# Two experts that begin with the first tokens, order edges on the transposes of experts' tokens, and the last two units tile by tile

## The chip, the cores and the metric

The kernel runs on one core of a Trainium2 chip. Its time is the device time of one execution in microseconds. A core has five engines, each with its own in-order queue of instructions: TensorE (PE, with its weight loads as PEld), VectorE (DVE), ScalarE (ACT), GpSimd (POOL) and SyncE (SP), which here only issues DMA transfers. GpSimd issues the indirect ones, gathers and scatters of rows. They wait for each other through semaphores.

## The reference, cut to what matters

Three layers follow each other on 2304 tokens of 512 features.

```python
# attention: 4 batches x 8 heads, 576 x 64; only the 32 largest scores of a row are kept
x = attention(q, k, v)                       # 2304 x 512
# dense layer
h = x @ w_in;  g = h * clip(h + 3, 0, 6) / 6
x = g @ w_out                                # 2304 x 2048 and back to 512
# mixture of 8 experts: each token goes to its two best by noisy logits
logits = x @ w_gate + log1p(exp(x @ w_noise)) * noise
top2, top2_w = two largest of each row, softmax over the two
for e in range(8):
    mask = tokens that chose e
    out[mask] += top2_w * (relu(x[mask] @ w1[e]) @ w2[e])    # 512 -> 1024 -> 512
```

## The kernel before, in words

The first part (`phase_a`) runs attention and the dense layer together, in steps written out by hand, for chunks of two token tiles of 128. A unit of the dense layer is one block of 128 of the 2048 inner features for one chunk: `mm1` (line 462, tile `h`, 12 matmuls), then a ReLU, a product and a split on ScalarE, VectorE and GpSimd, then `mm2` (line 502, tile `xa`, 6 matmuls). Weights of 11 of the 16 blocks are streamed again for every chunk (tag `ws`, 4 buffers, shared with the experts' raw weights `r`), five stay (tag `wr`, shared with the experts' converted weights). Every number is split into a rounded part and a remainder, so a product takes three matmuls. When a chunk is done, its tokens are routed (`make_route`): a small chain on GpSimd, VectorE and ScalarE ends in scatters of token numbers and gate weights into a table `idw` in memory (line 755), one region for each expert. The routing runs in groups of tiles; the last group is tiles 16 and 17.

The second part (`phase_b`) runs the experts. A job is one expert and a range of rows of its region: `jobs` holds (expert, first row, tiles). With EARLY = 1 there are nine: expert 0 with its first 384 rows (3 tiles), expert 0 with the next 256 (2 tiles), and experts 1 to 7 with 5 tiles each. A job below EARLY is *early*: it reads rows that the first 16 token tiles wrote and does not wait for the last two. A flag checks that every early expert has its 384 rows by then; otherwise a general path runs at the end.

A job has eight units, one for each block of 128 of the 1024 inner features. Unit `g` is made of: `wload` (two DMAs of 256 KB on SP, three units ahead), `wsplit` (a copy on ScalarE, line 859, and a subtraction, line 861, on VectorE for the first four jobs and on GpSimd for the others), `mm1` (line 875, tile `hb`, in one PSUM buffer of two banks, tag "s"), ReLU and low part into `hh` (lines 880 and 881), and `mm2` (line 895, tile `ac`, one accumulator bank for each token tile, three matmuls for each tile). A job's tokens come by `fetch`: a DMA reads `idw` (line 830), GpSimd gathers the rows (line 810) into one of two buffers `xg`, and `turn` (lines 841 to 845) transposes one tile: four transposes on TensorE, a copy on ScalarE, a subtraction on VectorE. `turn` of an early job uses the PSUM buffer "s", that of other jobs the bank "misc". In the program, `turn` of the next job's tile j stands in unit 3 + j of this one. `finish` scales the accumulators by the gate weight, adds what other jobs wrote (`old`, gathered from `out`), and scatters the rows to `out` (line 912); jobs below `fresh` need no `old`. From unit 20 on (`LOOK`) each unit also checks one or two pieces of `w_in` and `w_out` for very small values: a DMA of 256 KB and two VectorE instructions (lines 978 to 981), ordered behind that unit's low part.

The framework sets each engine's order: it simulates the program with a cost model, and gives a free engine the ready instruction that stands first in the program. `after(tc, o, before)` adds an edge for this order alone; on the chip nothing waits for it, but an engine's queue is in order.

Of the kernel before, what the change touches and what calls it, by code (L numbers as in the profile page):

```python
# [141 lines left out]
def phase_a(tc, pools, ident, q, k, v, w_in, w_out, X, thrs, wscr, stream, begin, on_chunk=None, slots=NSLOT, pace=None):  # L142
    nc = tc.nc
    wp, ap, mp, ps, dr = pools
# [295 lines left out]
    chunks = [list(range(t, min(t + 2, slots // 8))) for t in range(0, slots // 8, 2)]  # L440
    chunk_of = {t: (c, j) for c, ts in enumerate(chunks) for j, t in enumerate(ts)}
    W, HP, G, ACC = {}, {}, {}, {}

    def w_fetch(u):
        c, fb = u
# [7 lines left out]
    def mm1(u):  # L453
        c, fb = u
        n = 128 * len(chunks[c])
        w = W[u][:, :, 0:512].rearrange("p a (d f) -> p a d f", d=4)
        xt = XT[c]
        p = ps.tile([128, 512], F32, name=f"h{c}_{fb}", tag="h")
        m = 0
        for d in range(4):  # L460
            for a, b in ((0, 0), (0, 1), (1, 0)):
                nc.tensor.matmul(p[:, 0:n], w[:, a, d, :], xt[b][:, d, 0:n], start=(m == 0), stop=(m == 11))  # L462
                m += 1
        HP[u] = p

    R = {}

# [37 lines left out]
    XM, XW = {}, []  # L505
# [10 lines left out]
    fill = []  # L516
# [18 lines left out]
    for st in range(-6, end):  # L535
# [13 lines left out]
        s_, a, b, c, d, e, av_, x1, x2 = (st - x for x in (OS, OA, OB, OC, OD, OE, OV, OX, OY))  # L549
# [47 lines left out]
        while fill and room > 0:  # L597
            room -= fill[0][0]
            fill.pop(0)[1]()
    return fill, XW  # L600


NE, DF2 = 8, 1024
NF2 = DF2 // 128
# [2 lines left out]
CAP0 = 384  # L607
AHEAD = 3
LOOK = 20
EARLY = 1  # L610
DVE_JOBS = 4
NOID = 1 << 20
SCW = 2
# [6 lines left out]
def after(tc, o, before):  # L620
    tc.add_manual_dep(o.ins, before.ins.name, mybir.DependencyInfo(
        mybir.DependencyClass.NoSync, mybir.DependencyReason.SCHED_ONLY), reason="order")
# [159 lines left out]
    return on_chunk, scat, (nz, tok, logits, logits2, route)  # L782


def phase_b(tc, pools, ident, X, idw, w1, w2, out, early, late, looks):


    nc = tc.nc
    wp, bp, ps = pools
# [5 lines left out]
    XE, ID, ACC, WT, HH, RAW = {}, {}, {}, {}, {}, {}  # L795
    accs = ["pa", "av", "h", "xa0", "xa1"]
    xg = [bp.tile([128, NJ, DM], F32, name=f"xg{i}") for i in range(2)]
# [36 lines left out]
    def turn(job, j):  # L834
        xe = XE[job]
        if job < EARLY:
            pm = ps.tile([128, 2, 512], F32, name=f"et{job}_{j}", tag="s")[:, 0]
        else:
            pm = ps.tile([128, 512], F32, name=f"et{job}_{j}", tag="misc")
        for d in range(4):  # L840
            nc.tensor.transpose(pm[:, d * 128:(d + 1) * 128], xg[job % 2][:, j, d * 128:(d + 1) * 128], ident)  # L841
        pv = pm.rearrange("p (d n) -> p d n", d=4)
        sl = slice(j * 128, (j + 1) * 128)
        nc.scalar.copy(xe[:, 0, :, sl], pv)
        TT(xe[:, 1, :, sl], pv, xe.bitcast(F32)[:, 0, :, sl], op=ALU.subtract)  # L845
# [18 lines left out]
    def mm1(g):  # L864
        job, f = divmod(g, NF2)
        n = 128 * jobs[job][2]
        w = WT[g][:, :, 0:512].rearrange("p a (d f) -> p a d f", d=4)
        p = ps.tile([128, 2, 512], F32, name=f"hb{g}", tag="s")
        nh = 1 if n <= 512 else 2
        hn = n // nh  # L870
        for half in range(nh):
            m = 0
            for d in range(4):
                for a, b in ((0, 0), (0, 1), (1, 0)):
                    nc.tensor.matmul(p[:, half, 0:hn], w[:, a, d, :], XE[job][:, b, d, half * hn:(half + 1) * hn],  # L875
                                     start=(m == 0), stop=(m == 11))
                    m += 1
        h = bp.tile([128, 2, CAP], F32R, name=f"hh{g}", tag="hh", bufs=2)
        hv = h[:, :, 0:n].rearrange("p a (b n) -> p a b n", b=nh)
        nc.scalar.activation(hv[:, 0], p[:, 0:nh, 0:hn], AF.Relu)  # L880
        LOW[:] = [STT(hv[:, 1], p[:, 0:nh, 0:hn], 0.0,  # L881
                      h.bitcast(F32)[:, :, 0:n].rearrange("p a (b n) -> p a b n", b=nh)[:, 0],
                      op0=ALU.max, op1=ALU.subtract)]
        HH[g] = h

    def mm2(g):
        job, f = divmod(g, NF2)
        w = WT.pop(g)[:, :, 512:1024]
        h = HH.pop(g)
        prev = None  # L890
        for j in range(jobs[job][2]):
            if f == 0:
                ACC[job, j] = ps.tile([128, 512], F32, name=f"ac{job}_{j}", tag=accs[(j + 3 * (jobs[job][1] > 0)) % 5])
            for m, (a, b) in enumerate(((0, 0), (0, 1), (1, 0))):
                o = nc.tensor.matmul(ACC[job, j], h[:, a, j * 128:(j + 1) * 128], w[:, b, :],  # L895
                                     start=(f == 0 and m == 0), stop=(f == NF2 - 1 and m == 2))
                if g == N - 1:

                    if prev: after(tc, o, prev)
                    prev = o  # L900

    def finish(job):
        e, _, nj = jobs[job]
# [16 lines left out]
    N = len(jobs) * NF2  # L920
# [7 lines left out]
    for g in range(N):  # L928
        job, f = divmod(g, NF2)
# [247 lines left out]
def body(tc, q, k, v, w_in, w_out, w_gate, w_noise, noise, w1, w2, out, dbg=None):  # L1177
    nc = tc.nc
    with ExitStack() as ctx:
        cp = ctx.enter_context(tc.tile_pool(name="cp", bufs=1))  # L1180
        wp = ctx.enter_context(tc.tile_pool(name="wp", bufs=1))
        dr = ctx.enter_context(tc.tile_pool(name="dr", bufs=1, space=bass.MemoryType.DRAM))
        ps = ctx.enter_context(tc.tile_pool(name="ps", bufs=1, space=bass.MemoryType.PSUM))
        ident = cp.tile([128, 128], F32, name="ident")
        make_identity(nc, ident)
        thrs = cp.tile([128, NSLOT], F32, name="thrs")
        cnt = cp.tile([128, NE], F32, name="cnt")
        few = cp.tile([128, 1], F32, name="few")
        tiny = cp.tile([128, 64], F32, name="tiny") if w_in.dtype != F32 else None
        X = dr.tile([NTOK, DM], F32, name="X")  # L1190
        idw = dr.tile([NE * NTOK, 2], F32, name="idw")
        A = dr.tile([NTOK, DM], F32, name="A")
        wscr = dr.tile([NFB, 128, 2, 1024], F32, name="wscr")
        stream = set(fb for fb in range(NFB) if (fb * (NFB - NRES)) // NFB != ((fb + 1) * (NFB - NRES)) // NFB)
        with tc.tile_pool(name="mp", bufs=1) as mp:
            route, pace = [], []

            def begin():

                none = mp.tile([128, NE * NTOK // 128, 2], F32, name="none", tag="lx", bufs=LXB)  # L1200
                nc.gpsimd.memset(none, 0.0)
                nc.gpsimd.memset(none.bitcast(I32)[:, :, 1:2], NOID)
                nc.sync.dma_start(idw.rearrange("(p s) c -> p s c", p=128), none)
                route.extend(make_route(tc, (mp, ps), ident, idw, w_gate, w_noise, noise, cnt, few=few, pace=pace))
                zero = mp.tile([128, DM], F32, name="zero", tag="lx", bufs=LXB)
                nc.gpsimd.memset(zero, 0.0)
                for t in range(NT):
                    nc.sync.dma_start(out[t * 128:(t + 1) * 128, :], zero)
            with tc.tile_pool(name="ap", bufs=1) as ap:
                fill, xw = phase_a(tc, (wp, ap, mp, ps, dr), ident, q, k, v, w_in, w_out, X, thrs, wscr, stream,  # L1210
                                   begin, on_chunk=lambda *a: route[0](*a), pace=pace)
            for _, f in fill:
                f()
            t0 = GROUPS[-1][0]
            early, late = xw[:t0] + route[1][:2 * t0], xw[t0:] + route[1][2 * t0:]
            with tc.tile_pool(name="bp", bufs=1, reuse_waits="tile") as bp:
                looks = small_weights(tc, nc, bp, w_in, w_out, tiny) if tiny is not None else []
                phase_b(tc, (wp, bp, ps), ident, X, idw, w1, w2, out, early, late, looks)
        if dbg:
            for n, a in (("X", X), ("idw", idw)):  # L1220
                if n in dbg: nc.sync.dma_start(dbg[n], a)
            if "cnt" in dbg: nc.sync.dma_start(dbg["cnt"], cnt)
        fl = flags(nc, cp, ps, ident, thrs, cnt, few, tiny)
        some = nc.values_load(fl[0:1, 1:2], min_val=0, max_val=1)
        with tc.If(some > 0):
            row = nc.values_load(fl[0:1, 0:1], min_val=0, max_val=1)
            with tc.If(row > 0):
                with tc.tile_pool(name="gp", bufs=1) as gp:
                    general_x(tc, (wp, gp, ps, dr), ident, q, k, v, w_in, w_out, w_gate, w_noise, noise,
                              X, A, idw, wscr, cnt)  # L1230
            with tc.tile_pool(name="gp2", bufs=1) as gp:
                general_out(tc, (wp, gp, ps, dr), ident, X, idw, w1, w2, out)
# [27 lines left out]
```

## Time and profile before

| | us |
|---|---|
| median of 3 runs | 1424.24 (1422.05 to 1424.36) |
| the profiled execution | 1423.71 |
| its span, first to last instruction | 1421.9 |
| TensorE busy | 1342.9 (94%) |
| VectorE busy | 988.8 (70%) |
| GpSimd busy | 840.1 (59%) |
| ScalarE busy | 748.2 (53%) |

The dense layer ends and the experts begin around 900 to 925 us. In the rows further down, a timeline line has the start, the duration, the engine, the line of the kernel, the operation, output and inputs, shapes and count; in square brackets stands how long the engine sat idle before it and what ended that. Ends of matmuls are modelled. A line of the chain of waits has the start, the duration and the piece of work that the end of the program depended on there.

### The profile page before, as it was taken

How to read it: one execution, taken by the hardware profiler on the slowest of the kernel's cores; microseconds unless marked ns; L12 is line 12 of the kernel's file. 1: busy time of each engine (PE TensorE's matmuls, PEld its weight loads, DVE VectorE, ACT ScalarE, POOL GpSimd, SP SyncE). 2: the span in 40 equal slices, each digit the busy share in tenths (PEclk: the TensorE clock that was granted, in tenths of full speed). 3: DMA queues.
4: the chain of work that ended last, by engine and by line, in shares of the span. 5: the costliest groups of instructions: out<-in, count | busy, mean ns of one | idle time of the engine just before them, and what ended most of it. 6: DMA issues, size and time to landing. Idle time of an engine off the chain costs nothing.

```text
span 1421.9 us, 26937 instructions
## 1 busy us (share of the span) xinstructions
PE 1342.9 (94%) x9006; PEld 1135.2 (80%) x9006; DVE 988.8 (70%) x3805; ACT 748.2 (53%) x1565; POOL 840.1 (59%) x1173
## 2 busy tenths in 40 slices
PE   5778899999999999999999999799999999999996
PEld 3445688888888888888888888677989888888985
DVE  7999997899997889987899973245453524434241
ACT  6767767666667766665776654244322322222220
POOL 7756766666677787575676855135414556465461
PEclk8788999999999999999999999999999999999999
DMA  8676745434346463444334546657545555475431
GB/s 250 211 270 241 251 150 188 161 134 139 127 159 218 140 168 126 169 141 146 122 131 152 140 158 241 165 160 229 165 145 193 173 159 190 140 218 166 143 120 38
DMA packets 138099, 239.56 MB, mean 168 GB/s; under 512 B 39779, under 2 KB 93155, under 8 KB 123872
## 3 DMA queue, kind: packets, MB, share of 16 engines
q1 hardware_dynamic: 127600, 210.57, 45.2%
q0 software_dynamic: 10352, 27.18, 5.9%
q8 instruction: 73, 1.20, 0.3%
q14 instruction: 74, 0.61, 0.1%
HBM read 209.08 MB, written 31.64 MB: 169 GB/s over the span
## 4 chain that ended last, share of the span: by engine, by line
PE 79%; DVE 11%; POOL 3%; DMA 3%; issue 2%; ACT 1%; SPq 0%; POOLq 0%; DVEq 0%; ACTq 0%
PE hb L875 15%; PE ac L895 15%; PE h L462 13%; PE xa L502 12%; PE av L417 8%; PE s L294 5%; PE pa L383 4%; DVE e L364 2%; DVE seg L312 1%; PE et L841 1%; DVE wt L116 1%; DVE wraw L117 1%; POOL idw L755 1%; DVE a L351 1%; PE av L420 1%
## 5 line engine op out<-in xcount | busy, mean ns | idle before, releaser
L895 PE MATMUL ac<-w,hh 128*128 128x512 f32 x960 | 247.9, 400 | 7.4 <-ACT hh L880 7.3
L875 PE MATMUL hb<-xe,w 128*128 128x320 f32 (+2 forms) x1536 | 238.8, 310 | 1.1 <-DVE xe L845 0.4
L875 PEld LDWEIGHTS hb<-xe,w 128*128 128x128 f32 x1536 | 231.1, 188 | 9.9 <-issue 3.0
L345 POOL TENSOR_TENSOR y<-z,ss 128x576 f32<-128x576 bf16 x144 | 199.8, 1389 | 48.5 <-DVE z L339 45.0
L895 PEld LDWEIGHTS ac<-w,hh 128*128 128x128 f32 x960 | 173.2, 188 | 46.8 <-ACT hh L880 11.5
L881 DVE SCALAR_TENSOR_TENSOR hh<-hb,hh 128x640 fp32r<-128x640 f32 (+2 forms) x72 | 53.9, 749 | 218.0 <-ACT hh L880 210.6
L880 ACT ACTIVATE hh<-hb 128x640 fp32r<-128x640 f32 (+2 forms) x72 | 46.5, 646 | 290.5 <-PE hb L875 257.4
L312 DVE MAX8 seg<-ss 128x8 f32<-128x82 f32 (+1 forms) x1008 | 167.3, 229 | 35.6 <-ACT ss L303 34.7
L462 PE MATMUL h<-xT,ws 128*128 128x256 f32 x1188 | 167.1, 287 | 4.1 <-DVE r L477 4.0
L502 PE MATMUL xa<-ws,g 128*128 128x512 f32 x594 | 170.3, 406 | 0.0
L462 PEld LDWEIGHTS h<-xT,ws 128*128 128x128 f32 x1188 | 150.6, 190 | 10.8 <-DVE r L477 6.4
L861 POOL TENSOR_TENSOR w<-r,w 128x1024 fp32r<-128x1024 f32 x40 | 98.3, 2462 | 90.5 <-ACT w L859 83.2
L364 DVE SCALAR_TENSOR_TENSOR e<-ss,thrs,e 128x576 f32<-128x576 f32 x144 | 139.6, 969 | 0.2 <-issue 0.2
L417 PE MATMUL av<-pt,v 128*64 128x128 f32 (+1 forms) x1280 | 122.7, 279 | 5.3 <-ACT pt L398 3.6
L490 POOL TENSOR_TENSOR g<-r,g 128x256 fp32r<-128x256 f32 x124 | 98.5, 794 | 43.4 <-ACT g L186 37.0
L334 ACT ACTIVATE e<-ss,a 128x576 f32<-128x576 f32 x144 | 113.6, 790 | 13.0 <-POOL a L327 12.0
L351 DVE MAX8 a<-y 128x8 f32<-128x576 f32 x144 | 107.9, 749 | 16.7 <-POOL y L345 16.2
L303 ACT COPY ss<-s 128x576 f32<-128x576 f32 x144 | 92.8, 644 | 46.6 <-PE s L294 26.3
L398 ACT COPY pt<-pa 128x512 f32<-128x512 f32 x144 | 84.9, 590 | 60.9 <-PE pa L383 58.9
L339 DVE TENSOR_SCALAR_CACHE_REDUCE z<-ss,a 128x576 bf16<-128x576 f32 x144 | 115.4, 801 | 1.0
L502 PEld LDWEIGHTS xa<-ws,g 128*128 128x128 f32 x594 | 101.3, 189 | 16.5 <-issue 3.3
L417 PEld LDWEIGHTS av<-pt,v 128*64 128x64 f32 x1280 | 78.5, 139 | 44.2 <-issue 19.6
(195 smaller groups left out, 2655.4 us busy)
## 6 DMA issues: line engine op xcount, KB each, us to landing
ws<-wscr SPq DMA_DIRECT2D x99, 1024.0 KB
r<-in_moe_w_dram SPq DMA_DIRECT2D x144, 256.0 KB
wscr<-wsp SPq DMA_DIRECT2D x11, 1024.0 KB
wraw<-in_moe_w_in_dram SPq DMA_DIRECT2D x16, 512.0 KB
wraw<-in_moe_w_out_dram SPq DMA_DIRECT2D x16, 512.0 KB
ck<-in_moe_w_in_dram SPq DMA_DIRECT2D x32, 256.0 KB
ck<-in_moe_w_out_dram SPq DMA_DIRECT2D x32, 256.0 KB
out_dram<-zero SPq DMA_DIRECT2D x18, 256.0 KB
```

The source lines that it names most:

```text
L312: nc.vector.max(ST[i][:, j, :], SS[i][:, edge[j]:edge[j + 1]])
L334: nc.scalar.activation(e, SS[i], AF.Exp, bias=A8[i][:, 24:25], scale=0.125)
L339: TS(z, SS[i], A8[i][:, 7:8], None, op0=ALU.is_lt, op1=ALU.add, accum_out=A8[i][:, 26:27])
L345: nc.gpsimd.tensor_tensor(y, Z.pop(i), SS[i], op=ALU.mult)
L351: nc.vector.max(A8[i][:, 8:16], Y.pop(i))
L364: STT(E[i], SS.pop(i), thrs[:, i:i + 1], E[i], op0=ALU.is_ge, op1=ALU.mult, accum_out=SUM[i // 2][:, i % 2:i % 2 + 1])
L417: nc.tensor.matmul(o[half, row:row + n], vt, pt[:, row:row + n], start=(j == 0), stop=(j == 4), skip_group_check=True)
L462: nc.tensor.matmul(p[:, 0:n], w[:, a, d, :], xt[b][:, d, 0:n], start=(m == 0), stop=(m == 11))
L490: low = eng.tensor_tensor(g[:, 1, 0:n], R.pop(u)[:, 0:n], g.bitcast(F32)[:, 0, 0:n], op=ALU.subtract)
L502: nc.tensor.matmul(ACC[t], g[:, a, j * 128:(j + 1) * 128], w[:, b, :], start=(fb == 0 and m == 0), stop=(fb == NFB - 1 and m == 2))
L875: nc.tensor.matmul(p[:, half, 0:hn], w[:, a, d, :], XE[job][:, b, d, half * hn:(half + 1) * hn], start=(m == 0), stop=(m == 11))
L895: o = nc.tensor.matmul(ACC[job, j], h[:, a, j * 128:(j + 1) * 128], w[:, b, :], start=(f == 0 and m == 0), stop=(f == NF2 - 1 and m == 2))
```

## The change

EARLY becomes 2, so that there are ten jobs: experts 0 and 1 with their first 384 rows, experts 0 and 1 with the next 256, and experts 2 to 7 with 5 tiles. `fresh` becomes 1 by its formula: the second job reads `old`. The four jobs whose weights VectorE converts are now the four partial ones. Second, `mm1` of both parts keeps its last matmul in `lastmm` (that of unit 0 is left out), and each transpose of `turn` gets an order edge behind the one kept at that point of the program. Third, the second product of the last unit but one is left until that of the last, and both run tile by tile in a fixed order.

```diff
@@ phase_a
+    lastmm = []
...
-                nc.tensor.matmul(p[:, 0:n], w[:, a, d, :], xt[b][:, d, 0:n], start=(m == 0), stop=(m == 11))
+                o = nc.tensor.matmul(p[:, 0:n], w[:, a, d, :], xt[b][:, d, 0:n], start=(m == 0), stop=(m == 11))
                 m += 1
         HP[u] = p
+        lastmm[:] = [o]
...
-    return fill, XW
+    return fill, XW, lastmm
...
-EARLY = 1
+EARLY = 2
@@ phase_b, turn
-            nc.tensor.transpose(pm[:, d * 128:(d + 1) * 128], xg[job % 2][:, j, d * 128:(d + 1) * 128], ident)
+            o = nc.tensor.transpose(pm[:, d * 128:(d + 1) * 128], xg[job % 2][:, j, d * 128:(d + 1) * 128], ident)
+            after(tc, o, lastmm[0])
@@ phase_b, mm1
-                    nc.tensor.matmul(p[:, half, 0:hn], w[:, a, d, :], XE[job][:, b, d, half * hn:(half + 1) * hn],
+                    o = nc.tensor.matmul(p[:, half, 0:hn], w[:, a, d, :], XE[job][:, b, d, half * hn:(half + 1) * hn],
                                      start=(m == 0), stop=(m == 11))
                     m += 1
+        if g: lastmm[:] = [o]
@@ phase_b, mm2
-        w = WT.pop(g)[:, :, 512:1024]
-        h = HH.pop(g)
+        if g == N - 2: return
+
+        gs = [g - 1, g] if g == N - 1 else [g]
+        ws, hs = [WT.pop(x)[:, :, 512:1024] for x in gs], [HH.pop(x) for x in gs]
         prev = None
         for j in range(jobs[job][2]):
             if f == 0:
                 ACC[job, j] = ps.tile([128, 512], F32, name=f"ac{job}_{j}", tag=accs[(j + 3 * (jobs[job][1] > 0)) % 5])
-            for m, (a, b) in enumerate(((0, 0), (0, 1), (1, 0))):
-                o = nc.tensor.matmul(ACC[job, j], h[:, a, j * 128:(j + 1) * 128], w[:, b, :],
-                                     start=(f == 0 and m == 0), stop=(f == NF2 - 1 and m == 2))
-                if g == N - 1:
-
-                    if prev: after(tc, o, prev)
-                    prev = o
+            for x, w, h in zip(gs, ws, hs):
+                for m, (a, b) in enumerate(((0, 0), (0, 1), (1, 0))):
+                    o = nc.tensor.matmul(ACC[job, j], h[:, a, j * 128:(j + 1) * 128], w[:, b, :],
+                                         start=(x % NF2 == 0 and m == 0), stop=(x % NF2 == NF2 - 1 and m == 2))
+                    if g == N - 1:
+                        if prev: after(tc, o, prev)
+                        prev = o
```

## Rows read from the trace of the kernel before

**Rows 1.** Waits of TensorE, 850 us on: total us, times, longest us
```profile
PE et L841 <- DMA xg<-X,id: 10.1, 2, 7.2
```

**Rows 2.** Windows: length, busy us of PE, PEld, DVE, ACT, POOL, clock, DMA share, GB/s
```profile
0.00:100.00 100.00, 69.80 (x338) 44.72 (x338) 91.06 (x309) 72.40 (x145) 71.08 (x116) 0.85 0.78 260
...
902.00:922.00 20.00, 12.79 (x71) 11.61 (x71) 6.08 (x11) 5.17 (x11) 3.06 (x3) 0.83 0.50 156
...
975.00:1000.00 25.00, 24.99 (x163) 21.93 (x162) 14.89 (x20) 12.74 (x20) 7.25 (x5) 1.00 0.69 221
```

**Rows 3.** Timeline of TensorE at the end of the dense layer
```profile
888.94 1.58 PE L462 MATMUL h<-xT,w 128*128 128x256 f32 x12
...
891.83 1.67 PE L462 MATMUL h<-xT,ws 128*128 128x256 f32 x12
...
909.26 1.11 PE L841 MATMUL et<-ident,xg 128*128 128x128 f32 x4 [7.21 <-DMA xg<-X,id]
910.02 2.91 PE L462 MATMUL h<-xT,ws 128*128 128x256 f32 x12
```

**Rows 4.** Chain of waits up to the first transposes
```profile
900.99 2.86 DMA id<-idw
...
904.90 4.32 DMA xg<-X,id
```

**Rows 5.** Timeline, one turn: its transposes and its last VectorE instruction
```profile
916.19 0.60 PE L841 MATMUL et<-ident,xg 128*128 128x128 f32 x4
...
917.45 0.69 DVE L845 TENSOR_TENSOR xe<-et,xe 128x512 fp32r<-128x512 f32 x1
```

**Rows 6.** Timeline of TensorE, first products of expert 0 (3 tiles, then 2)
```profile
922.19 2.25 PE L875 MATMUL hb<-xe,w 128*128 128x384 f32 x12
...
951.51 2.28 PE L875 MATMUL hb<-xe,w 128*128 128x384 f32 x12
...
955.89 2.25 PE L875 MATMUL hb<-xe,w 128*128 128x384 f32 x12
...
963.72 2.33 PE L875 MATMUL hb<-xe,w 128*128 128x384 f32 x12
...
969.12 0.28 PE L875 MATMUL hb<-xe,w 128*128 128x256 f32 x1
...
973.19 1.68 PE L875 MATMUL hb<-xe,w 128*128 128x256 f32 x12 [0.21 <-DVE hh L881]
```

**Rows 7.** Timeline of TensorE, units of two tiles
```profile
989.61 1.59 PE L875 MATMUL hb<-xe,w 128*128 128x256 f32 x12
...
992.71 1.58 PE L875 MATMUL hb<-xe,w 128*128 128x256 f32 x12
```

**Rows 8.** Chain of waits, a unit of five tiles near the end
```profile
1395.35 3.53 PE hb L875 x24
1398.88 3.49 PE ac L895 x15
```

**Rows 9.** VectorE: a two-tile unit's conversion (timeline), the checks (groups, 1020 to 1057)
```profile
992.79 1.23 DVE L861 TENSOR_TENSOR w<-r,w 128x1024 fp32r<-128x1024 f32 x1 [0.71 <-ACT w L859]
...
L981 DVE SCALAR_TENSOR_TENSOR cu<-cu 128x256 f32<-128x256 f32 x5 | 2.0, 421 | 0.1
...
L980 DVE TENSOR_SCALAR cu<-ck 128x256 int32<-128x256 int32 x5 | 1.3, 284 | 0.0
```

**Rows 10.** DMA issues: expert weights and checked pieces, KB each
```profile
r<-in_moe_w_dram SPq DMA_DIRECT2D x144, 256.0 KB
...
ck<-in_moe_w_in_dram SPq DMA_DIRECT2D x32, 256.0 KB
```

**Rows 11.** Timeline and chain of the tail: low part, last VectorE product, last scatter
```profile
1399.66 0.82 DVE L881 SCALAR_TENSOR_TENSOR hh<-hb,hh 128x640 fp32r<-128x640 f32 x1 [6.20 <-ACT hh L880]
...
1410.90 0.76 DVE y L911
...
1414.33 0.97 POOL L912 DMA_INDIRECT out_dram<-y,id  x1 [0.30 <-issue]
```

More of the change, by code (lines that the diff above doesn't have):

```diff
@@ L782, in make_route, with phase_b @@
     return on_chunk, scat, (nz, tok, logits, logits2, route)
-def phase_b(tc, pools, ident, X, idw, w1, w2, out, early, late, looks):
+def phase_b(tc, pools, ident, X, idw, w1, w2, out, early, late, looks, lastmm):
     nc = tc.nc
@@ L1209, in body @@
             with tc.tile_pool(name="ap", bufs=1) as ap:
-                fill, xw = phase_a(tc, (wp, ap, mp, ps, dr), ident, q, k, v, w_in, w_out, X, thrs, wscr, stream,
+                fill, xw, lastmm = phase_a(tc, (wp, ap, mp, ps, dr), ident, q, k, v, w_in, w_out, X, thrs, wscr, stream,
                                    begin, on_chunk=lambda *a: route[0](*a), pace=pace)
@@ L1217, in body @@
                 looks = small_weights(tc, nc, bp, w_in, w_out, tiny) if tiny is not None else []
-                phase_b(tc, (wp, bp, ps), ident, X, idw, w1, w2, out, early, late, looks)
+                phase_b(tc, (wp, bp, ps), ident, X, idw, w1, w2, out, early, late, looks, lastmm)
         if dbg:
```

## The prediction

> **What bounds the kernel now.** I read the waits of TensorE first, then the stages, then the order of its instructions. From 850 us on, the longest wait of TensorE is one of 7.2 us, for gathered token rows, out of 10.1 us in two places [rows 1]. The stage table puts the larger one between 902 and 922 us: 12.8 us of work in 20, at a mean granted clock of 0.83, while later stages run full at 1.00 [rows 2]. The order of TensorE's queue shows why: the first four transposes of the experts' tokens stand in the queue at 909.26, ahead of three units of the dense layer that wait for nothing, and nothing passes them [rows 3]. Their data comes from a chain that TensorE can't hasten: the index read is issued at 900.99 and takes 2.86 us, the gather goes out at 904.90 and lands 4.32 us later, at 909.2 [rows 4]. The second wait, 2.9 us, stands before the unit at 963.72: it starts 7.83 us after the one before, where its neighbours take 4.38 [rows 6]. There the rows of the last two token tiles were late. Beyond that TensorE is full until the tail, so any stretch with thinner units costs what its TensorE time and its slowest helper cost.
>
> **The change, part by part.** Times are those of the profiled execution: 1423.71 us, of which the span is 1421.9. The median of the three runs is 1424.24, so 0.53 is added at the end.
>
> *Order edges, first use.* The transposes of job 0 now stand behind the last first-product of the dense layer. From 902.05 TensorE goes straight on: a unit takes 2.89 us (888.94 to 891.83) [rows 3], the three that are left have their first products done 2 x 2.89 + 1.5 later, at 909.3, with six second-product matmuls each beside them. The gathered rows land at 909.2: no wait, but no margin. One turn (four transposes, ScalarE's copy, VectorE's subtraction) takes from 916.19 to 918.14, 1.95 us [rows 5], and three turns share one PSUM buffer, so they run one after the other: 909.3 + 3 x 1.95 = 915.2 at best. Queueing behind weight conversions on VectorE (1.23 us each [rows 9]) adds up to 3 x 2.3 with ScalarE's; I take 917 for the first expert product, against 922.19 [rows 6]: **-5.2** (bounds -7 and 0). The slow clock after the long wait goes with it: 12 matmuls took 2.91 us at 910.02 where they take 1.58 at 888.94 [rows 3]; this is inside the 5.2, since I counted full-speed units.
>
> *First units of job 0.* From 922.19 to 951.51 five units take 29.3 us, 7.4 more than 5 x 4.38 [rows 6]: routing products of the last tiles, and a wait for ScalarE, which converts weights that all arrive then. With the dense layer done earlier, weight buffers come free before the turns, and the routing transposes can fill TensorE's idle time between turns. I take 4.4 in place of 7.4: **-3.0** (0 to -4).
>
> *Second early expert.* Routing of the last tiles now has 16 units instead of 8 to hide in, so the 7.83 - 4.38 = 3.4 us go. The two job changes near it (969.12 - 963.72 = 5.40 and 973.19 - 969.12 = 4.07 for units that run in 4.38 and 3.10 [rows 6, 7]) lose 2.0 now; the two changes that take their place reuse the same three accumulators and need `old` for the second, whose gather runs 30 us ahead; I give them 0.5 each. Together **-4.4** (-2.4 to -5). What is late next here is nothing on TensorE's path by my count: late rows landed at 963, job 2 will begin some 90 us after 909.
>
> *The price of the split.* Expert 1 runs as 8 units of three tiles and 8 of two instead of 8 of five: 4.38 + 3.10 against 3.53 + 3.49 = 7.02 [rows 6 to 8], 0.46 x 8 = **+3.7**. Its weights are read and converted twice (8 x 512 KB; 8 x 1.23 us on VectorE).
>
> *Turns of job 1 in the PSUM pair of the first products.* Before, they used another bank. A three-tile unit occupies the pair for 2.28 of its 4.38 us and then until its ReLU and low part are read [rows 6]; a turn holds it 1.95 us more [rows 5]. If all of it fits into the 2.1 us left: 0 each; if it comes on top and behind a conversion of 1.23: 3.2 each. The ReLU takes about half of the 2.1, so I take 1.2 x 3 = **+3.5** (0 to 9.6).
>
> *Weight checks in thin units.* From unit 20 on, 16 checks fall in 12 two-tile units, which before fell in five-tile units. On VectorE a check is 0.28 + 0.42 us and fits the 0.71 us in which VectorE waits for ScalarE [rows 9]; two checks in a unit overrun it slightly: 0.5 in all. On the DMA queues these 12 units need 12 x 512 KB of weights, 16 x 256 KB of checks [rows 10] and some nine gathers and scatters of 256 KB: 12.8 MB in 12 x 3.10 + 1.1 = 38.3 us, 335 GB/s. The two-tile units at 975 to 1000 us ran without a stall at 221 GB/s and 0.69 of the DMA engines [rows 2]; scaled, 335 would be 1.05, so 1.9 us over. Bounds: 0 if the lead of three units absorbs it; at the 260 GB/s of the kernel's first 100 us, the highest stretch of that length [rows 2], 49.4 us, +11.1. I take **+2.5** in all, nearest to the row of the same kind of unit.
>
> The Trainium skill, page "DMA: Bandwidth & Descriptors", section "Where 436 GB/s comes from", puts the limit of reads from memory at about 358 GB/s per core; by that figure, an estimate, the stretch needs 35.9 us and this term would be 0.5, the sum 2 us lower. No row read here shows more than 260, so I don't use it.
>
> *Later transposes.* In the five-tile jobs the turn of the last tile now stands in the last unit of the job before. After the hidden product come 15 second-product matmuls, 3.49 us [rows 8], over a turn of 1.95 [rows 5]: **0** (up to 0.5 at each of 6 changes, +3). Moving e1 and e2's conversions to GpSimd puts them where the five-tile units already have them: 0.
>
> *The tail.* The last but one second product moves behind the last first product. That product waits only until the ReLU and low part before it are read: the product before ended at 1398.88 [rows 8], its low part at 1400.48 [rows 11]; five older matmuls and three of the new order (3.49 / 15 = 0.233 each, 1.9 us) cover that. So it runs 1400.75 to 1404.28, its low part is ready 1.6 later at 1405.9, the first tile is done at 1406.1, and 24 matmuls finish at 1411.7. The last VectorE product ends 0.78 later and the last scatter starts at 1412.55, not 1414.33: tiles now come every 1.4 us, and GpSimd, at 0.97 + 0.30 us a scatter, no longer lags [rows 11]. **-1.7** (-2.2 to +0.5, if the wait for the low part is longer and nothing covers it).
>
> Sum: -5.2 - 3.0 - 4.4 + 3.7 + 3.5 + 2.5 + 0 - 1.7 = -4.6; 1423.71 - 4.6 = 1419.1, and 1419.6 beside the median.
>
> **The rivals.**
> *Thin units starve (slower).* Sixteen thin units in a row, twelve of them with checks, run at what the DMA queues deliver. For it: 335 GB/s are needed and the highest stretch shows 260. Against it: there the DMA share was only 0.78 [rows 2], and three units of lead. With +11.1 for +2.5 the sum is +4.0: 1428.2. It makes the kernel slower from about 267 GB/s down, where the twelve units take 48 us.
> *The head gains nothing.* The three serial turns, behind conversions on both helpers, put the first expert product at 922 again, or the clock falls there. For it: one PSUM buffer, now without dense units to cover the turns. Against it: during the wait of before both helpers stood idle as well. Without the 5.2: 1424.8, no change.
> *The edges don't do what they say.* They fix an order, not an arrival. The margin at 909.3 is nil; if the gather lands 3 us later, because the dense layer's loads are closer to it, TensorE waits there again, 3 us: 1422.6, no change.
> *More than summed.* If the turns of job 1 fit and the DMA queues keep up, 3.5 + 2.5 go: 1413.6.
>
> **How the numbers follow.** Forecast with its neighbours 0.42 (own range 1416 to 1423), more than summed 0.15, the head 0.16, the edges 0.09, thin units 0.18. A measurement of this kernel tells 0.2%, 2.85 us, from no change. Faster: 0.15 and most of the 0.42, 0.54; slower: thin units and a tail of the head's case, 0.21; the same: 0.25. The range takes the best bounds without their extremes and the starving case: 1412 to 1429.
>
> **What would show it.** Right: no wait for gathered rows on TensorE after 850; the first expert product near 917; a clock of 0.95 or more from 905 to 925; the first product of e2 near 1050.7, 2.9 earlier than before; the last scatter 0.9 us after TensorE's last matmul, and 1.7 less of tail in all. Wrong: VectorE or ScalarE waiting for weights in the two-tile units, units of the second job at 6 us and more, or a wait of TensorE for transposes at each job's change.

## The result, and the profile after

The changed kernel is slower: 1439.64 us (median of 4 runs, 1436.21 to 1441.32) against 1424.3 (4 runs, 1422.05 to 1427.56), a ratio of 1.0116 (95% interval 1.0093 to 1.0139). The forecast was 1419.6, faster, in a range of 1412 to 1429: wrong in sign and outside its range. The profiled execution took 1436.21 us, with a span of 1434.1 and a mean clock of 0.977 (before: 0.975), so TensorE's clock over the whole span is not the cause.

I cut both spans at three places: the first expert product, the change from three-tile to two-tile units, and the first product of e2, from which on both kernels do the same units.

| stage | before, us | after, us |
|---|---|---|
| start to first expert product | 922.19 | 920.64 |
| from there to e2's first product | 131.4 | 144.5 (79.3 in three-tile units, 65.2 in two-tile units) |
| from there to the end of the span | 368.3 | 369.0 |

The loss is all in the middle. First, the waits of TensorE from 850 us on, in the kernel after (total us, times, longest us), to be read against [rows 1]:

```profile
PE ac L902 <- ACT hh L884: 9.2, 12, 1.3
PE hb L878 <- DVE hh L885: 6.5, 4, 2.8
...
PE hb L878 <- DVE xe L848: 2.1, 3, 0.7
...
PE et L843 <- DMA xg<-X,id: 0.7, 1, 0.7
```

The wait that the change was to remove is gone: 10.1 us for gathered rows [rows 1] are 0.7. In its place stand waits for `hh`, the low part of the hidden product, of up to 2.8 us; the list does not say why VectorE was late with it. The timeline of all engines in the two-tile units, kernel after, does, here for a wait of 2.02 us:

```profile
1021.12 0.38 ACT L884 ACTIVATE hh<-hb 128x256 fp32r<-128x256 f32 x1 [1.58 <-PE hb L878]
...
1023.62 0.29 DVE L986 TENSOR_SCALAR cu<-ck 128x256 int32<-128x256 int32 x1 [2.82 <-DMA ck<-in_moe_w_in_dram]
...
1024.30 0.42 DVE L885 SCALAR_TENSOR_TENSOR hh<-hb,hh 128x256 fp32r<-128x256 f32 x1
...
1024.77 2.63 PEld L878 LDWEIGHTS hb<-xe,w 128*128 128x128 f32 x12 [2.45 <-DVE hh L885]
1024.77 2.93 PE L878 MATMUL hb<-xe,w 128*128 128x256 f32 x12 [2.02 <-DVE hh L885]
```

The ReLU was done at 1021.50. The low part that follows it, 0.42 us of work, began at 1024.30, because a weight check ahead of it in VectorE's queue stood 2.82 us for its DMA; TensorE had 2.02 us without work behind that, and then ran twelve matmuls in 2.93 us where 1.57 is usual; the granted clock from 1021 to 1026 was 0.87. Windows of the same kernel (length; busy us of PE, PEld, DVE, ACT, POOL; clock; DMA share; GB/s) show what the DMA engines did then, to be read against the last line of [rows 2]:

```profile
1011.00:1016.00 5.00, 5.00 (x35) 4.41 (x35) 3.24 (x7) 3.07 (x5) 2.90 (x3) 1.00 0.52 155
1016.00:1021.00 5.00, 5.00 (x34) 4.28 (x33) 4.39 (x9) 2.21 (x4) 4.08 (x4) 1.00 0.99 339
1021.00:1026.00 5.00, 2.98 (x12) 2.02 (x11) 1.06 (x4) 1.43 (x2) 1.67 (x2) 0.87 1.06 360
```

In 1016 to 1026 they were full, at 339 and 360 GB/s. The Trainium skill, page "DMA: Bandwidth & Descriptors", section "Where 436 GB/s comes from", gives about 358 GB/s as the limit that memory sets to one core's transfers between memory and SBUF. The 339 and 360 GB/s here lie near it, but the kernel before moved 381 GB/s, reads and writes together, from 70 to 90 us, so the traces don't bear it out as a limit.

VectorE's groups between 1003 and 1066, kernel after (count | busy us, mean ns of one | idle before), answer to [rows 9]:

```profile
L987 DVE SCALAR_TENSOR_TENSOR cu<-cu 128x256 f32<-128x256 f32 x14 | 10.1, 726 | 0.3
L986 DVE TENSOR_SCALAR cu<-ck 128x256 int32<-128x256 int32 x15 | 7.7, 520 | 11.9 <-DMA ck<-in_moe_w_in_dram 11.9
```

There is a second thing to see here. Beside the 11.9 us of waiting, the same instructions are longer than before: means of 520 and 726 ns against 284 and 421, some 7.8 us in all (15 x 0.236 + 14 x 0.305). Waiting does not lengthen an instruction. The timeline around the longest of TensorE's waits, 2.83 us, kernel after, shows what ran beside the long ones:

```profile
1050.25 4.74 POOL L864 TENSOR_TENSOR w<-r,w 128x1024 fp32r<-128x1024 f32 x2
...
1051.57 1.22 DVE L986 TENSOR_SCALAR cu<-ck 128x256 int32<-128x256 int32 x1 [2.58 <-DMA ck<-in_moe_w_in_dram]
1052.83 2.45 DVE L987 SCALAR_TENSOR_TENSOR cu<-cu 128x256 f32<-128x256 f32 x1
...
1055.67 2.93 PE L878 MATMUL hb<-xe,w 128*128 128x256 f32 x12 [2.83 <-DVE hh L885]
```

The check's second instruction, which took 0.42 us at 1023.95, ended at 1055.28, 0.29 us after GpSimd's second weight conversion, and the low part stood behind it. Experiments 7 and 9 test whether the conversions are the cause. The trace of the kernel before has the same thing:

```profile
1119.03 3.25 DVE L980 TENSOR_SCALAR cu<-ck 128x256 int32<-128x256 int32 x1
...
1119.69 2.42 POOL L861 TENSOR_TENSOR w<-r,w 128x1024 fp32r<-128x1024 f32 x1
```

In that kernel, over all 64 checks, the means are 540 and 520 ns. The 284 and 421 of [rows 9] are from a stretch in which GpSimd converts nothing.

The head, TensorE's timeline of the kernel after, answers to [rows 3, 5, 6]:

```profile
908.49 0.65 PE L843 MATMUL et<-ident,xg 128*128 128x128 f32 x4 [0.67 <-DMA xg<-X,id]
...
912.71 0.60 PE L843 MATMUL et<-ident,xg 128*128 128x128 f32 x4
...
914.98 0.62 PE L843 MATMUL et<-ident,xg 128*128 128x128 f32 x4
...
920.64 4.19 PE L878 MATMUL hb<-xe,w 128*128 128x384 f32 x12
...
942.37 2.35 PE L878 MATMUL hb<-xe,w 128*128 128x384 f32 x12 [0.71 <-DVE xe L848]
...
948.80 2.35 PE L878 MATMUL hb<-xe,w 128*128 128x384 f32 x12 [0.71 <-DVE xe L848]
```

From the first transposes to the first product 12.1 us pass, not the 3 x 1.95 of the forecast. The third turn alone takes 5.3 us, and ScalarE's timeline shows why: its transposes end at 915.60, and its copy stands last in this list.

```profile
915.86 1.04 ACT L862 CAST w<-r 128x1024 fp32r<-128x1024 f32 x1 [1.43 <-DMA r<-in_moe_w_dram]
916.81 0.59 ACT L512 ACTIVATE xm<-xa 128x512 f32<-128x512 f32 x1
917.34 1.05 ACT L862 CAST w<-r 128x1024 fp32r<-128x1024 f32 x1
918.29 0.58 ACT L664 COPY lx<-lt 128x512 f32<-128x512 f32 x1
918.77 0.59 ACT L847 CAST xe<-et 128x512 fp32r<-128x512 f32 x1
```

For 3.2 us the copy stood behind two weight conversions, one of them held up by its DMA, and two steps of the last tokens. The units with a turn of job 1 lie 6.43 us apart (942.37 to 948.80), where 4.38 is usual. Two windows of the same kernel, the same columns as above, show the clock and the DMA engines there:

```profile
905.00:925.00 20.00, 14.27 (x70) 11.88 (x68) 9.40 (x13) 9.90 (x16) 4.13 (x5) 0.85 1.01 342
...
922.00:930.00 8.00, 8.00 (x38) 7.63 (x38) 1.37 (x5) 2.70 (x5) 1.68 (x7) 0.77 0.40 134
```

### The profile page after: what moved, and what is told of

It reads as the page before. It is cut to its first block, busy times and chain, and to the rows that moved or that the text cites. A ratio compares the mean times of both kernels' runs of the same rounds, so it can differ in the third digit from the quotient of the medians.

```text
span 1434.1 us, 27037 instructions
## 1 busy us (share of the span) xinstructions
PE 1347.2 (94%) x9006; PEld 1133.5 (79%) x9006; DVE 1010.5 (70%) x3813; ACT 757.4 (53%) x1581; POOL 854.8 (60%) x1183
## 4 chain that ended last, share of the span: by engine, by line
PE 73%; DVE 12%; DMA 4%; issue 4%; POOL 3%; ACT 2%; SPq 1%; POOLq 0%; DVEq 0%; ACTq 0%
PE h L463 13%; PE hb L878 13%; PE xa L504 13%; PE ac L902 12%; PE av L417 7%; PE s L294 5%; PE pa L383 4%; DMA ck<-in_moe_w_in_dram 2%; DVE e L364 2%; DVE seg L312 2%; DVE a L351 1%; DVE wt L116 1%; DVE wraw L117 1%; POOL w L864 1%; PE av L420 1%
## 5 line engine op out<-in xcount | busy, mean ns | idle before, releaser
L902 PE MATMUL ac<-w,hh 128*128 128x512 f32 x960 | 252.8, 402 | 10.5 <-ACT hh L884 9.2
L878 PE MATMUL hb<-xe,w 128*128 128x320 f32 (+2 forms) x1536 | 245.6, 313 | 9.0 <-DVE hh L885 6.5
L878 PEld LDWEIGHTS hb<-xe,w 128*128 128x128 f32 x1536 | 235.9, 191 | 20.1 <-DVE hh L885 8.1
L864 POOL TENSOR_TENSOR w<-r,w 128x1024 fp32r<-128x1024 f32 x48 | 115.6, 2422 | 92.6 <-ACT w L862 87.0
L862 ACT CAST w<-r 128x1024 fp32r<-128x1024 f32 x80 | 84.0, 1050 | 52.6 <-issue 23.2
```

Of the source, the lines that this page charges most:

```text
L864: eng.tensor_tensor(w[:, 1], r, w.bitcast(F32)[:, 0], op=ALU.subtract)
L878: o = nc.tensor.matmul(p[:, half, 0:hn], w[:, a, d, :], XE[job][:, b, d, half * hn:(half + 1) * hn], start=(m == 0), stop=(m == 11))
```

## Experiments

Each ratio is to the kernel before, run on the same chip; intervals are 95%. Stage times are from one profiled execution each, whose start to the first expert product varies by some us from run to run; so I compare stages, not positions.

**1. Checks later.** The checks begin at unit 32, after the two-tile units, and come faster there.

```
-LOOK = 20
+LOOK = 32
-        looks, now = looks[1 + (g % 3 == 0):], looks[:1 + (g % 3 == 0)]
+        looks, now = looks[1 + (g % 2 == 0):], looks[:1 + (g % 2 == 0)]
```

> The changed kernel, with the weight checks beginning at unit 32 (the first unit of five tiles) in place of 20, at 1.5 pieces per unit in place of 1.33. Theory (the check transfers do not arrive in time in the thin units, and VectorE stands behind them): the 16 units of two tiles take 51 to 53 us in place of the 65.2 of the changed kernel, no VectorE wait for a checked piece before the fifth job, and the time falls by 11 to 14 us, to 1425 to 1428. Rival A (the thin units starve on their own weights, read twice): they stay at 60 us or more and the time above 1434. Rival B (checks cost what they cost anywhere): the loss moves into the units of five tiles, and the time stays within 4 us of the changed kernel.

Measured: 1427.69 against 1426.77, ratio 1.0004 (0.998 to 1.0027). The sixteen two-tile units take 52.1 us (65.2 after), with no wait for `ck` in them. The checks in the thin units are what makes the change slower; in five-tile units they cost nothing that shows (369.2 us from e2's first product to the end of the span, against 369.0 after).

**2. One early expert**, with the edges and the new tail kept (`EARLY = 2` back to `EARLY = 1`).

> The changed kernel with EARLY = 1: one early expert as before, but order edges and the last two units tile by tile kept. Theory (the loss is in the sixteen units of two tiles with checks, and in the turns of job 1 in the PSUM pair): both go, the gain at the head (1.5 us) and of the tail (1.9 us) stays, and the 2.9 us wait for the last tokens goes because routing starts earlier: 1416 to 1422, the first five-tile unit of expert 2 at 1046 to 1051 us. Rival (the order edges cost by themselves, because transposes come later): 1428 or more, with waits of first products for transposed tokens at changes of job.

Measured: 1431.39, ratio 1.0038 (1.0018 to 1.0057): a miss. TensorE's timeline of this kernel shows a wait of 7.12 us before the turns of job 1, where the kernel before has the 2.9 us wait for late rows and the kernel after none:

```profile
956.70 1.11 PE L843 MATMUL et<-ident,xg 128*128 128x128 f32 x4 [7.12 <-DMA xg<-X,id]
957.46 2.91 PE L902 MATMUL ac<-w,hh 128*128 128x512 f32 x6
960.17 2.95 PE L878 MATMUL hb<-xe,w 128*128 128x384 f32 x12
```

The turns of job 1 now belong to the last token tiles, whose routing ends in a gather that lands at 956.7; the turn stands after the fifth unit and everything behind it waits. In the kernel after, job 1 needs only early tokens, so the second early expert hides this wait, as forecast.

**3. No edges**, two early experts (`after(tc, o, lastmm[0])` left out after the transposes).

> The changed kernel without the order edge on the transposes; two early experts and the tail kept. Theory (edges are worth little here, since serial turns eat what the wait gave; the loss is in the thin units): the wait for gathered rows of 6 to 8 us is back near 902 us, the first expert product is at 920 to 923 us, the thin units are as slow as in the changed kernel, and the time is 1434 to 1442. Rival (the edges are what costs): 1430 or less.

Measured: 1452.58, ratio 1.0175 (1.0131 to 1.0219): a miss, slower than expected. The waits of TensorE from 850 us on, this kernel:

```profile
PE et L843 <- DMA xg<-X,id: 27.3, 5, 8.9
```

Without the edges the transposes are put ahead of ready products in five places. With two early experts the edges are worth some 0.6% (1.0175 against 1.0116; the two intervals just overlap).

**4. The tail alone**, on the kernel before.

> The kernel before, with nothing but the last two units tile by tile. Theory: everything up to the last first product but one is as before; the last scatter is issued 1.5 to 2 us earlier counted from the first product of expert 2; the time falls by 1.5 to 2 us, to 1422.5, at the edge of what three rounds can tell. Rival (the wait of the last matmuls for the low part eats it): the same last scatter within 0.5 us.

Measured: 1425.83, ratio 0.9998 (0.9966 to 1.0029): no gain that can be measured. The last scatter starts at 1411.73, 356.9 us after e2's first product (before: 360.8, so 3.9 earlier, where 1.5 to 2 were expected), but the span ends 9.6 us after that start, where before it ends 7.6 after. More in 12.

**5. Turns in another bank.** Experiment 1, and the turns of job 1 no longer use the PSUM pair of the first products.

```
-        if job < EARLY:
+        if job == 0:
             pm = ps.tile([128, 2, 512], ...
```

> The kernel with late checks (checks from unit 32 on), and the turns of job 1 in the bank misc in place of the PSUM pair of the first products. Theory (each turn in the pair lengthens a three-tile unit from 4.4 to 6.4 us, as the changed kernel's first products at 942.4, 948.8 and 955.2 show): the three units with turns take 4.6 to 5 us, 4 to 6 us go, and the time is 1421 to 1424. Rival (the units are held by VectorE's and ScalarE's order, not by the bank): they stay at 6 us or more and the time within 2 us of the kernel with late checks (1427.7).

Measured: 1418.16 against 1420.6, ratio 0.9982 (0.997 to 0.9993): faster than the kernel before. TensorE's first products of the second and third unit with a turn, and of the unit after them:

```profile
947.32 2.25 PE L878 MATMUL hb<-xe,w 128*128 128x384 f32 x12
951.94 2.25 PE L878 MATMUL hb<-xe,w 128*128 128x384 f32 x12
956.56 2.25 PE L878 MATMUL hb<-xe,w 128*128 128x384 f32 x12
```

4.62 us apart, where they were 6.43. The pair cost 1.8 us a turn.

**6. Deeper buffers for the checks** (`ck` with 3 buffers for 2), otherwise the kernel after.

> The changed kernel with three buffers for the checked pieces in place of two; the order on TensorE, ScalarE and GpSimd is unchanged. Theory (the DMA engines are full in the thin units, 335 to 360 GB/s wanted): the 16 two-tile units still take 60 us or more, and the time is 1435 or more; a buffer only moves the wait. Rival (the piece is asked for too late, and a buffer more hides its way): 56 us or less, and 1431 or less.

Measured: 1433.79, ratio 1.009 (1.007 to 1.011); the thin units take 63.4 us. The waits for `ck` there fall from 11.9 to 2.9 us, but the time comes back in one unit of 11.53 us. Its timeline, GpSimd and VectorE:

```profile
1050.17 9.33 POOL L864 TENSOR_TENSOR w<-r,w 128x1024 fp32r<-128x1024 f32 x4
1051.67 7.98 DVE L986 TENSOR_SCALAR cu<-ck 128x256 int32<-128x256 int32 x1
```

A check of 0.28 us took 7.98, until 0.15 us after the last of GpSimd's weight conversions, which ran one after the other. So the waits for transfers fell as the rival said, and the thin units stayed long as the theory said, but through this hold-up, not through transfers alone.

**7. Checks without their traffic.** All 64 checks look at the first two pieces, which stay in SBUF; the other 62 pieces are not read.

> The changed kernel with all 64 checks on VectorE at their places, but only two pieces of the weights read, which every check uses (so the flag covers two pieces only). Theory (transfers, not VectorE's work): the 16 two-tile units take 52 to 56 us, the rest from VectorE standing behind GpSimd's weight conversions in the last three of them, and the time is 1426 to 1430. Rival (VectorE's own time for two checks in a unit of 3.1 us, and GpSimd's port): 60 us or more, 1434 or more.

Measured: 1431.89, ratio 1.008 (1.0058 to 1.0102); the thin units take 60.7 us, not the 52 to 56 expected. Twelve of them run in 3.1 to 3.4 us, the two at the changes of job in 3.7 and 3.9, the last in 4.4, and one takes 10.41. The timeline around it:

```profile
1047.57 7.54 DVE L990 TENSOR_SCALAR cu<-ck 128x256 int32<-128x256 int32 x1
1047.96 7.00 POOL L864 TENSOR_TENSOR w<-r,w 128x1024 fp32r<-128x1024 f32 x3
...
1055.50 0.69 DVE L848 TENSOR_TENSOR xe<-et,xe 128x512 fp32r<-128x512 f32 x1
...
1056.24 1.11 PE L843 MATMUL et<-ident,xg 128*128 128x128 f32 x4 [5.75 <-DVE xe L848]
```

With no DMA to wait for, the check began 0.39 us before three GpSimd conversions and ended 0.15 us after the last of them; the low part of a token tile stood behind it, and TensorE waited 5.75 us. So there are two causes: traffic, worth 65.2 - 60.7 = 4.5 us, and GpSimd's conversions holding VectorE up. The Trainium skill, page "SBUF — State Buffer", section "🔬 SBUF: two separate sides", says that VectorE and GpSimd share a pair of ports under an exclusive lock, held for a whole instruction, against some kinds of VectorE instruction. The trace agrees that one blocks the other, and shows it lasting over three instructions in a row.

**8. Two turns of job 0 in one pair**, one bank each, on experiment 5, so that the second turn need not wait for the first one's reads.

```
+            if j != 1: PAIR[:] = [ps.tile([128, 2, 512], ...)]
+            pm = PAIR[0][:, j % 2]
```

> The kernel with late checks and the turns of job 1 in misc, and the first two turns of job 0 share one allocation of the PSUM pair, one bank each, so that their transposes need not wait for each other. Theory (the three serial turns, 11.7 us from the first transposes to the first expert product in the changed kernel, keep the head from gaining): 2 to 4 us shorter, the first expert product that much nearer to the first transposes, and the time 1418 to 1422. Rival (ScalarE's and VectorE's queues, with weight conversions between, set the pace): within 1 us of the same head and of the kernel with the turns of job 1 in misc.

Measured: 1418.85 against 1420.6, ratio 0.9988 (0.9977 to 0.9999). From the first transposes to the first product 11.2 us, against 10.7 in experiment 5: the shared buffer is not what makes the head long. (One profile each; over all kernels with edges this stretch is 10.3 to 12.4 us.)

**9. GpSimd's first conversions back to VectorE.** The weights of units 32 to 34, which are converted during the last thin units, on the kernel after.

```
-eng = nc.vector if (g // NF2 < DVE_JOBS or jobs[g // NF2][1]) else nc.gpsimd
+eng = nc.vector if (g < DVE_JOBS * NF2 + AHEAD or jobs[g // NF2][1]) else nc.gpsimd
```

> The changed kernel, with the conversions of units 32 to 34 on VectorE in place of GpSimd, so that no GpSimd conversion falls among the thin units; TensorE's and ScalarE's orders are unchanged. Theory (two causes in the thin units: late transfers of about 4.5 us and VectorE's checks standing behind GpSimd's conversions, about 8 us; the kernel without traffic showed one check of 7.5 us beside three conversions of 7.0 us): no check instruction above 0.6 us in the thin units, these 16 units take 56 to 60 us in place of 65.2, and the time falls by 5 to 8 us, ratio to the kernel before 1.005 to 1.008. Rival (it is the transfers alone, and the check stood behind late data): 63 us or more, ratio 1.010 or more.

Measured: 1432.08 against 1422.36, ratio 1.0072 (1.0047 to 1.0097); thin units 59.8 us. VectorE's waits for `ck` between 999 and 1066:

```profile
DVE cu L986 <- DMA ck<-in_moe_w_in_dram: 9.7, 8, 2.6
```

As expected in time: taking away the conversions gives 5.4 us, and the waits for `ck` stay. One check instruction of 2.63 us is left, against the 0.6 that was expected at most; it starts at 1061.41, beside a GpSimd conversion of 2.36 us that starts at 1061.40. Traffic (4.5) and conversions (5.4) add to 9.9 of the 13.1 us that experiment 1 gives back; the other 3.2 were not separated. The two causes overlap: in experiment 7, without traffic, the one unit beside the conversions lies 7.3 us above 3.10, and without that excess its thin units would take 53.4 us, an estimate, near the 52.1 of experiment 1. No run took both away and kept the checks.

**10. One early expert with later turns.** Experiment 2, with the turns of job 1 from the seventh unit of job 0 on in place of the fourth.

```
+        s = 6 if job == 0 else 3
-        if f >= 3 and nxt and f - 3 < nxt[2]: turn(job + 1, f - 3)
+        if f >= s and nxt and f - s < nxt[2]: turn(job + 1, f - s)
```

> One early expert with order edges and the tail (the kernel that took 1.0038 of the time before), and the two turns of job 1 three units later, in units 6 and 7 of job 0. Theory (that kernel lost 7.1 us in front of the turns of job 1, which the edge let in as early as unit 4, while the rows of the last tokens land 36 us after the head): that wait is below 1 us, 5 to 8 us go, ratio 0.997 to 1.000. Rival (the wait is set by the routing chain and only moves to the first product of job 1): a wait of 4 us or more remains there, ratio 1.002 or more.

Measured: 1416.86 against 1422.36, ratio 0.9968 (0.9954 to 0.9982). TensorE's timeline, where experiment 2 waited 7.12 us:

```profile
953.71 0.60 PE L843 MATMUL et<-ident,xg 128*128 128x128 f32 x4
955.54 2.25 PE L878 MATMUL hb<-xe,w 128*128 128x384 f32 x12
958.33 0.60 PE L843 MATMUL et<-ident,xg 128*128 128x128 f32 x4
```

No wait. From the first expert product to expert 1's first five-tile unit it takes 65.9 us (921.61 to 987.54); the kernel before takes 73.6 (922.19 to 995.80). The edges' gain is had without the split of expert 1 and without thin units under the checks.

**11. Turns ahead of conversions.** Experiment 5, with each turn of job 0 put, in the program, before one of the first three weight conversions.

```
     wload(g)
-    wsplit(g)
 for j in range(jobs[0][2]):
     turn(0, j)
+    wsplit(j)
```

> The kernel with late checks and the turns of job 1 in misc (0.9982 of the time before), with each turn of job 0 in front of one of the first three weight conversions in the program, in place of all three conversions before the turns. Theory (the serial turns take 3.5 to 3.9 us each, not 1.95, because conversions of 1.05 and 1.23 us stand between on ScalarE and VectorE): from the first transposes to the first expert product 7 to 9 us in place of 10.7, 2 to 3 us less in all, ratio 0.996 to 0.9975. Rival (the first product then waits for its own weights): the same 10 to 11 us, ratio 0.998 or more.

Measured: 1418.35 against 1422.36, ratio 0.9977 (0.9965 to 0.9989). From the first transposes (909.01) to the first product (920.05) 11.0 us, against 10.7 in experiment 5: a miss, but no test of the theory. On the chip ScalarE, VectorE and TensorE have the same order there as in experiment 5: the framework, which sets the order, took no turn ahead of a conversion. So this is experiment 5 measured again, on another chip (0.9977 and 0.9982), and a head with the turns ahead was not run. In ScalarE's queue the third turn's copy still has two conversions, two `xm` and one `lx` between it and the second's.

**12. Experiment 10 with the old tail.**

> The kernel with one early expert, the edges and the turns of job 1 from the seventh unit on (e10), with the tail of the kernel before put back. Theory: the new tail starts the last scatter about 1.9 us earlier and gives 2 to 2.4 of it back between the start of the last scatter and the end of the span (10.0 us with the new tail, 7.6 with the old), so the time is that of e10 within what can be measured: 0.995 to 0.998 of the kernel before, with 7.4 to 7.8 us from the start of the last scatter to the end of the span. Rival: the new tail carries part of e10's gain, the 1.9 us are real and the long end belongs to something else: 0.998 to 0.9995, and an end of about 10 us here too.

Measured: 1414.4 against 1418.21, ratio 0.9969 (0.9953 to 0.9985), the same as experiment 10. Its last two scatters:

```profile
1402.75 0.97 POOL L916 DMA_INDIRECT out_dram<-y,id  x1 [0.30 <-issue]
1404.03 0.97 POOL L916 DMA_INDIRECT out_dram<-y,id  x1 [0.30 <-issue]
```

The span ends at 1411.6, 7.6 us after the start of the last scatter, as before; with the new tail it is 9.5 to 10.2 in every kernel profiled with it. So the new tail gives nothing that can be measured here, in experiment 4 or between 10 and 12 (the intervals leave room for some 3 to 4 us), and the gain of experiment 10 is that of the edges and the place of the turns. The later turns without the edges were not run, so these two are not separated. Both versions beat the kernel before and the kernel after.

## Why the prediction was wrong, step by step

- *No wait for gathered rows; no wait for the last tokens*: right. 0.7 us is left of 10.1, and the late tokens' wait of [rows 6] is gone. In experiment 2 (edges, one early expert) a wait of 7.1 us stays, in experiment 3 (two early experts, no edges) 27.3 us in all; experiment 10 shows that edges and later turns do it with one early expert too.
- *Head, -5.2*: it gave -1.55 (922.19 to 920.64). What it had wrong is the 1.95 us of a turn, whose row [rows 5] was read where ScalarE took the copy at once. Here the expert weights, the last tokens' results of the dense layer and the turns come together: between 905 and 925 us the DMA share is 1.01, the turns are 4.2 and 2.3 us apart, and the third takes 5.3 us, 3.2 of them in ScalarE's queue (see the timeline above). Routing products that wait for ScalarE stand in front of the first expert product as well. The rival "the head gains nothing" was nearer. The expected clock of 0.95 was 0.85, and in 922 to 930 us 0.77, after a stretch of single transposes with gaps; the first product took 4.19 us for 2.25. A second bank for the turns (8) does not shorten it; that ScalarE's order sets it is read from the trace, and no run has changed that order.
- *First units of job 0, -3.0*: too careful. The first three take 6.32, 4.66 and 4.33, 2.2 over 3 x 4.38, and the next ones are lengthened by turns alone, so 7.4 became 2.2: -5.2, beyond the bound of -4.
- *Turns of job 1 in the PSUM pair, +3.5*: mis-sized. Three units of 6.43, each 2.05 above 4.38: +6.2, inside the bounds; experiment 5 isolates 1.8 each. My rule that the ReLU takes half of the 2.1 us left was too kind.
- *Weight checks in thin units, +2.5*: the step that failed. Sixteen thin units took 65.2 us, where 16 x 3.10, a job change of 0.5 and this term give 52.6: 12.6 us beyond it. I counted VectorE's time and the DMA rate each by itself, against a mean over 38 us. But VectorE takes its queue in order: a check whose 256 KB are late holds the low part that TensorE needs next, so a burst is paid for (339 to 360 GB/s in 1016 to 1026) though the mean of 1008 to 1040 was only 264. And the check itself was costed at 0.28 + 0.42 us beside any work, from rows in which GpSimd converted nothing.
- *Moving e1 and e2's conversions to GpSimd, 0*: wrong twice. Only e2's move; e1's two jobs are partial and stay on VectorE. And e2's first stand in the last thin units, where VectorE has checks to run; experiment 9 puts 5.4 us on them, experiment 7, without traffic, 7.3. "The five-tile units already have them" was true, and there too a check took up to 3.25 us, but those units have 7 us each to lose some in.
- *Tail, -1.7*: right to the last scatter (358.9 us after e2's first product, before 360.8: -1.9) and wrong at the end, since 2.5 us come back behind it: 7.6 us from the last scatter's start to the end of the span become 10.1.

Of the forecast's first product of e2, 1050.7, 14.4 us are missed: 3.65 in the head, 12.6 in the thin units, 0.8 in the three-tile units, less 2.6 by which my sum of differences stood above the same sum built from units. With 2.4 of the tail that is 16.8 of the 17.1 us between 1419.1 and the profiled 1436.21. The rival "thin units starve" had the right stage and a price of 11.1 where 15.1 were measured (65.2 less 49.6 and 0.5); it was refused for a DMA share of 0.78 and three units of lead, and it named the rate, not the queue order behind a late check or behind GpSimd. Its 260 GB/s were a mean over 100 us and no ceiling: the same trace holds 381 over 10 us (below).

## What to carry to other kernels

Optional work that stands in an in-order queue ahead of work the bound engine needs costs its own lateness, not its own duration: put it where the unit is long, and judge its transfers by the burst, not the mean. A duration read where an engine's neighbour was idle is a lower bound; before moving work to GpSimd look at what VectorE runs at that moment. An edge that holds a transpose behind ready products pays only as long as its data arrives by the new place; moving the turn three units later was worth at least as much as a second early expert with its two repairs (0.9968 against 0.9982 in experiment 5; the intervals overlap), and needed no split.

## What the runs showed of the hardware

- A VectorE `TENSOR_SCALAR` of 0.28 us took 7.54 and 7.98 us beside back-to-back GpSimd conversions (experiments 7 and 6), and ended 0.15 us after the last of them.
- The DMA engines were full (share 0.99 to 1.06) at 339 to 381 GB/s; the mean of the first 100 us of the kernel before, 260 at 0.78, hides this window of it (columns as above):

```profile
80.00:90.00 10.00, 8.01 (x57) 5.50 (x55) 9.84 (x43) 8.44 (x19) 5.52 (x9) 1.00 1.05 381
```

- With the old tail (last scatters some 1.29 us apart) the last bytes move sooner after the last scatter than with the new one (1.40 us apart). Windows of the kernel after, from the start of its last scatter at 1424.00 (columns as above):

```profile
1425.00:1426.00 1.00, 0.00 (x0) 0.00 (x0) 0.00 (x0) 0.00 (x0) 0.00 (x0) 1.00 0.50 176
1426.00:1427.00 1.00, 0.00 (x0) 0.00 (x0) 0.00 (x0) 0.00 (x0) 0.00 (x0) 1.00 0.24 84
1427.00:1428.00 1.00, 0.00 (x0) 0.00 (x0) 0.00 (x0) 0.00 (x0) 0.00 (x0) 0.72 0.07 25
1428.00:1429.00 1.00, 0.00 (x0) 0.00 (x0) 0.00 (x0) 0.00 (x0) 0.00 (x0) 0.50 0.03 8
```

The kernel before, whose last scatter starts at 1414.33, is done sooner:

```profile
1416.00:1417.00 1.00, 0.00 (x0) 0.00 (x0) 0.00 (x0) 0.00 (x0) 0.00 (x0) 0.50 0.54 203
1417.00:1418.00 1.00, 0.00 (x0) 0.00 (x0) 0.00 (x0) 0.00 (x0) 0.00 (x0) 0.50 0.00 0
```

Its last bytes move within 2.7 us of that start, those of the kernel after up to 5.0 us after it, the last ones at 8 to 25 GB/s. Why they straggle was not found.
